# Another order for the same instructions of a one-core transformer block: per-slot scheduling settings changed for slots 0 to 9 and 18 to 31

## The chip, the core and the metric

One core of a Trainium2 chip runs the whole program. Its engines work at the same time and each takes its instructions strictly in the order in which the program lists them: TensorE (PE in the profile) multiplies matrices, ScalarE (ACT) evaluates functions, VectorE (DVE) does elementwise work, GpSimd (POOL) small extras, SyncE (SP) starts transfers. They meet at semaphores only. The metric is the device time of one execution in microseconds (us). The profile records one such execution.

## What is computed

A pre-norm attention layer and a gated feed-forward layer on 2048 tokens of width 640, with 32 heads of 20:

```python
qkv = (x @ wqkv) -> q, k, v                       # x is layernorm(A_x)
scores = einsum("bhqd,bhkd->bhqk", q, k) * 20 ** -0.5
p = softmax(scores);  o = einsum("bhqk,bhkd->bhqd", p, v)
h = A_x + o.reshape(B, S, D) @ wo
g = layernorm(h) @ w_gate;  u = layernorm(h) @ w_up      # 640 -> 1728
h2 = h + (gelu(g) * u) @ w_down
```

The only other input, `B_x`, is not read. The costly part is the softmax: 32 heads x 2048 x 2048 exponentials.

## The kernel before

**Tiles.** Scores are made transposed, 128 keys by up to 512 queries, one PSUM bank each; 2048 such tiles in all. The queries are cut into eight chunks (512, five of 256, two of 128). A *slot* is a chunk with one or more groups of four heads; there are 32 slots: 0 to 7 are the first chunk, 8 to 11 the second, and so on, 28 and 29, 30 and 31 the two short chunks at the end.

**Who takes the exponential.** ScalarE takes two or three tiles with one instruction, in 716 *units* (452 of 128x1024 and 264 of 128x1536, writing `pts` or, for the second part of the same ring of buffers, `rege`). The units alternate between PSUM banks 0 to 2 and 3 to 5. In nearly every slot three groups of four tiles, and in all 352 tiles, go to VectorE instead: a `TENSOR_SCALAR` reads a score tile from its bank (L1148), and after four tiles four more of 128x2048 (L476) make from it four terms whose sum stands for the exponential. A VectorE tile is put in the third bank of a unit that has only two ScalarE tiles (a *third bank* in the change's title), or in a free background bank, and then its score matmul is an instruction of its own behind the unit's.

**TensorE's rows.** L1267 are the score matmuls (`ps<-qt_all,kt_all`), L1212 the products of probabilities and values ("PV"; they read `pts`, `rege` or `qt_all` and `v_all`), L1051 the value projections and L902 the projections of queries and keys, L1015 a bound for the softmax, L873 (with `regw`, `wo` or `wda`) L1526 and L1613 the output projection and the feed-forward layer, L1371 a transpose. L1642 are filler matmuls with a zero operand, in groups of four, and `L476 MATMUL ps<-kt_all` another filler: the planner puts them where it expects TensorE to idle.

**VectorE's other rows.** L1059 writes projected values to `v_all`, L907 projected queries and keys, L1019 the bound, L1350 copies the finished sums of a slot out of PSUM, L1377 and L1381 normalize them, L1475, L1552 to L1618 belong to the output projection and the feed-forward layer.

**What sets the order.** Nothing in the source lists the engines' orders. Each operation is recorded with an engine, a duration, a priority and its dependencies, and a list scheduler (`Sched.schedule`) replays the program once on paper and writes down for each engine the order in which operations became startable. Score matmuls and exponentials have the highest priority, PV comes next, and projections and the feed-forward layer fill what is left. Some thresholds of the scheduler have a value for each slot, picked by `at`, which indexes the tuple with the slot of the unit that was scheduled last:

- `QK_LEAD`: how early before the current exponential ends TensorE is kept free for the next score matmuls;
- `PE_AGE`: how long an operation must have been startable before TensorE takes it though it needs another array layout than the last one;
- `SD_AGE`, `SD_ROW`: how long a VectorE tile's own score matmul is held back;
- `RESV`: how long a bank is kept free for such a tile;
- `SHUFFLE`: a number that holds some low-priority operations back by up to 1 us, and so deals the order anew.

```python
at = lambda v: v[cur] if isinstance(v, tuple) else v
```

Two more tuples are read by the planner of units, before the scheduler runs: `D_RING[t]`, out of how many of a slot's VectorE tiles the third bank may be used, and `D_FIRST[t]`, the unit with which a slot's VectorE tiles begin:

```python
nd = 4 * len(d_kb[t])
...
ring[-1] = n == 3 and (i + 1) * D_RING[t] // nd > i * D_RING[t] // nd
```

`nd` is the number of VectorE tiles of slot `t`, 12 in slots 1 to 27.

Of the kernel before, what the change touches and what calls it, by code (L numbers as in the profile page):

```python
# [18 lines left out]
DRAIN = {"pe": 0.165, "act": 0.118, "dve": 0.085, "pool": 0.05, "sp": 0.0}  # L19
WARM_WIN, WARM_MIN = 3.4, 0.5  # L20
PAD_WIN, PAD_MIN = 3.4, 0.42
QK_LEAD = (0.6, 0.68, 0.45, 0.6, 0.65, 0.68, 0.55, 0.68, 0.82, 0.55, 0.72, 0.68, 0.6, 0.72, 0.72, 0.76, 0.55, 0.55, 0.65, 0.55, 0.65, 0.65, 0.76, 0.6, 0.6, 0.5, 0.6, 0.68, 0.6, 0.72, 0.76, 0.6,)
ACT_GAP = .012
PE_AGE = (0.5, 1.5, 2.5, 8.0, 1.5, 3.0, 2.5, 0.5, 2.5, 0.5, 5.0, 3.0, 2.0, 8.0, 3.0, 0.5, 2.5, 5.0, 1.5, 5.0, 1.5, 5.0, 5.0, 5.0, 2.0, 1.0, 1.0, 3.5, 8.0, 3.0, 5.0, 1.5,)
SD_AGE = (0.3, 0.6, 1.4, 0.8, 0.2, 0.6, 0.6, 0.6, 0.3, 0.0, 0.0, 1.4, 0.6, 1.0, 0.2, 0.0, 0.3, 0.8, 0.1, 0.2, 0.2, 0.8, 0.0, 0.0, 0.0,) + (0.5,) * 4 + (0.1, 0.2, 0.3,)
SD_ROW = (0, 1.0, 1.5, 0.6, 0.6, 0.6, 1.5, 1.0, 0.3, 1.5, 1.5, 1.5, 1.0, 1.5, 1.0, 0.6,) + (1.0,) * 4 + (0.6, 0.3, 0, 1.0, 1.0, 0.6, 1.0, 0.6, 1.5, 1.5, 0.6, 1.5,)
STOP = None


# [28 lines left out]
class Sched:  # L58
# [49 lines left out]
    def schedule(self):  # L108
# [29 lines left out]
        while done < total:  # L138
# [6 lines left out]
            for e in ENGINES:  # L145
# [8 lines left out]
                while ready[e]:  # L154
                    p, i = heapq.heappop(ready[e])
                    o = ops[i]
                    got = []
                    if e == "pe" and p[0] >= 1 and at(SHUFFLE) and o.i * at(SHUFFLE) % 37 < 3 and t < o.ready + 0.999:
                        skipped.append((p, i))
# [249 lines left out]
D_SPAN = (15, 18, 17,) + (18,) * 9 + (17, 16, 18, 17, 18, 17, 18, 17, 18, 17, 17,) + (16,) * 8 + (17,)
P33 = (2, 3, 4, 5)  # L410
# [44 lines left out]
def bass_sequential_preLN__mha_block__glu_gated_geglu__prompt_kernel(  # L455
# [12 lines left out]
    with ExitStack() as es:  # L468
# [609 lines left out]
        for s_, (c, gs) in enumerate(slots):  # L1078
# [6 lines left out]
        rem = [x for x in tiles if x[1:3] not in d_kb[x[0]]]  # L1085
        n_units = [(64 - 4 * D_SLOT[s_] + D_RING[s_] * D_SLOT[s_] / max(D_SLOT[s_], 1)) / 2.5 for s_ in range(len(slots))]
        d_first = [D_FIRST[s_] if s_ and CHUNKS[slots[s_][0]][0] // 512 in (CHUNKS[slots[s_ - 1][0]][0] // 512, 3) else max(0, D_FIRST[s_])
                   for s_ in range(len(slots))]
        for _ in range(2):
# [5 lines left out]
            while left:  # L1095
# [7 lines left out]
                for t, k in ((s_, in_slot[s_]), (s_ + 1, in_slot[s_] - n_units[s_])):  # L1103
# [628 lines left out]
```

## Time and profile before

| | us |
|---|---|
| median of 3 runs (lowest, highest) | 867.15 (865.39, 867.15) |
| the profiled execution, whole | 865.97 |
| its span in the trace | 864.3 |
| ScalarE busy in the span | 828.1 (96%) |
| TensorE busy in the span | 825.5 (96%) |
| VectorE busy in the span | 734.3 (85%) |

The granted TensorE clock is full over the whole span. 1.7 us of the profiled execution lie outside its span. From 30 us to 825 us ScalarE takes one exponential after the other; before that stand the first layernorm and projections, behind it the last chunk's feed-forward layer. A row of the timeline gives start, busy time, engine, source line, operation, output and inputs, and in brackets how long the engine was idle before it and what ended that.

### The profile page before, as it was taken

The page shows a single profiled execution, that of the slowest core. Times are in us where ns is not written, and L with a number is a line of the kernel's source. Part 1 is how long each engine was busy: PE and PEld are TensorE (multiplying, and loading weights), DVE is VectorE, ACT ScalarE, POOL GpSimd, SP SyncE. Part 2 cuts the span into 40 slices and gives each one's busy share as a digit, 9 for nine tenths or more (in the row PEclk, how much of TensorE's full clock was granted, in tenths as well). Part 3 has the DMA queues.
Part 4 walks back from the last instruction along what each step waited for, and adds up shares of the span by engine and source line. Part 5 has one row for each costly group of instructions (what it writes and reads, how often), then busy time and mean ns, then how long its engine had stood idle before and what let it go on. Part 6 is the DMA issues. An engine that isn't in the chain of part 4 may idle for free.

```text
span 864.3 us, 35997 instructions
## 1 busy us (share of the span) xinstructions
PE 825.5 (96%) x16372; PEld 412.6 (48%) x16372; DVE 734.3 (85%) x1382; ACT 828.1 (96%) x794; POOL 96.0 (11%) x275
## 2 busy tenths in 40 slices
PE   8999999999999999999989999999999999999998
PEld 7442333322343444445545455445445555666667
DVE  7788999888899897878879799999999899867434
ACT  6899899999999999999999999999999999899992
POOL 8001110110002110021102110001101110010000
PEclk9999999999999999999999999999999999999999
DMA  8211132124235400012101100011002101020000
GB/s 276 77 45 53 46 85 76 52 79 98 69 116 139 119 16 6 23 43 51 44 6 32 39 26 24 10 42 37 18 16 37 46 8 31 20 48 10 3 19 17
DMA packets 52160, 43.23 MB, mean 50 GB/s; under 512 B 22660, under 2 KB 47264, under 8 KB 52008
## 3 DMA queue, kind: packets, MB, share of 16 engines
q1 hardware_dynamic: 52008, 40.93, 17.4%
q8 instruction: 129, 2.11, 1.0%
q14 instruction: 23, 0.19, 0.1%
HBM read 27.95 MB, written 10.26 MB: 44 GB/s over the span
## 4 chain that ended last, share of the span: by engine, by line
ACT 64%; PE 24%; DVE 8%; issue 0%
ACT pts L476 44%; ACT rege L476 19%; PE ps L1267 6%; PE ps L1212 5%; PE ps L873 3%; PE ps L1526 3%; PE ps L902 3%; DVE rege L476 2%; PE ps L1051 1%; DVE qt_all L476 1%; DVE rege L1148 1%; DVE qt_all L1148 1%; ACT qt_all L476 1%; PE ps L1613 1%; DVE qt_all L1564 1%; DVE regw L476 0%
## 5 line engine op out<-in xcount | busy, mean ns | idle before, releaser
L476 ACT ACTIVATE pts<-ps 128x1024 bf16<-128x1024 f32 (+1 forms) x506 | 564.3, 1260 | 6.7 <-PE ps L1212 4.4
L1267 PE MATMUL ps<-qt_all,kt_all 32*128 32x256 bf16 (+2 forms) x4096 | 286.0, 273 | 18.5 <-ACT pts L476 8.7
L476 ACT ACTIVATE rege<-ps 128x1024 bf16<-128x1024 f32 (+1 forms) x210 | 247.7, 1272 | 3.2 <-PE ps L1212 2.1
L1267 PEld LDWEIGHTS ps<-qt_all,kt_all 32*128 32x128 bf16 x4096 | 92.7, 92 | 208.7 <-ACT pts L476 117.5
L1148 DVE TENSOR_SCALAR rege<-ps 128x512 int16<-128x512 f32 x220 | 148.6, 682 | 17.0 <-PE ps L1267 16.2
L1212 PE MATMUL ps<-rege,v_all 128*21 128x256 bf16 (+2 forms) x2226 | 135.5, 287 | 1.6 <-issue 0.7
L873 PE MATMUL ps<-rege,regw 128*32 128x256 bf16 (+1 forms) x2600 | 122.5, 296 | 6.0 <-ACT rege L476 1.5
L1212 PE MATMUL ps<-pts,v_all 128*21 128x256 bf16 (+2 forms) x2414 | 120.5, 273 | 0.2
L1148 DVE TENSOR_SCALAR qt_all<-ps 128x512 int16<-128x512 f32 x132 | 89.6, 684 | 12.4 <-PE ps L1267 11.8
L476 DVE TENSOR_SCALAR rege<-rege 128x2048 int16<-128x2048 int16 x141 | 95.3, 690 | 3.9 <-PE ps L1212 3.2
L873 PEld LDWEIGHTS ps<-rege,regw 128*32 128x32 bf16 x2600 | 59.7, 96 | 39.7 <-issue 18.7
L1212 PEld LDWEIGHTS ps<-rege,v_all 128*21 128x21 bf16 x2226 | 53.2, 91 | 40.9 <-issue 22.2
L1212 PEld LDWEIGHTS ps<-pts,v_all 128*21 128x21 bf16 x2414 | 55.1, 91 | 30.0 <-issue 22.2
L873 PE MATMUL ps<-regw,rege 128*32 128x320 bf16 x1296 | 66.4, 301 | 1.1 <-DVE rege L1618 0.5
L1212 PE MATMUL ps<-qt_all,v_all 128*21 128x256 bf16 (+1 forms) x1376 | 60.9, 264 | 1.3 <-DVE qt_all L476 1.2
L476 DVE TENSOR_SCALAR qt_all<-qt_all 128x2048 int16<-128x2048 int16 (+1 forms) x98 | 60.4, 630 | 1.5 <-PE ps L1212 0.7
L902 PE MATMUL ps<-regw 128*128 128x512 bf16 x190 | 57.4, 384 | 1.0 <-DVE rege L1148 0.5
L476 POOL TENSOR_SCALAR rn<-rc 128x16 int32<-128x16 int32 x22 | 7.0, 318 | 433.6 <-DMA rc<-sums 433.5
L476 DVE TENSOR_SCALAR qt_all<-rege 128x2048 int16<-128x2048 int16 x80 | 53.7, 682 | 1.1 <-PE ps L1212 0.7
L873 PEld LDWEIGHTS ps<-regw,rege 128*32 128x32 bf16 x1296 | 29.2, 96 | 18.6 <-issue 10.8
L1526 PE MATMUL ps<-rege,regw 128*128 128x128 bf16 (+1 forms) x420 | 37.7, 238 | 0.4 <-DVE rege L1574 0.2
L476 DVE TENSOR_SCALAR rege<-qt_all 128x2048 int16<-128x2048 int16 x52 | 35.6, 685 | 0.6 <-PE ps L1212 0.4
(166 smaller groups left out, 794.9 us busy)
## 6 DMA issues: line engine op xcount, KB each, us to landing
bsum<-rsums SPq DMA_DIRECT2D x88, 64.0 KB, 2.0
rege<-in_A_x_dram SPq DMA_DIRECT2D x4, 640.0 KB, 7.1
q_rows<-regw SPq DMA_DIRECT2D x20, 128.0 KB, 1.8
out_dram<-rege SPq DMA_DIRECT2D x15, 160.0 KB, 1.9
rege<-in_A_x_dram SPq DMA_DIRECT2D x7, 320.0 KB, 3.0
regw<-in_B_w_gate_dram SPq DMA_DIRECT2D x5, 432.0 KB, 3.1
regw<-in_B_w_up_dram SPq DMA_DIRECT2D x5, 432.0 KB, 3.3
kt_all<-k_rows SPq DMA_DIRECT2D x12, 160.0 KB
```

The costliest lines, as they stand in the source:

```text
L476: return lambda eng: getattr(eng, method)(*args, **kwargs)
L873: return [lambda eng, j=j: eng.matmul(out()[32 * j:32 * j + 32], l[:, 32 * j:32 * j + 32], r, start=start, stop=stop, tile_position=(0, 32 ...
L902: w_readers.append(op("pe", lambda eng, a=a: eng.matmul(bank(bk).rearrange("p (t s) -> p t s", s=128), wqk[:, a, col + 128 * t:col + 128 * ...
L1051: w_readers.append(op("pe", lambda eng, i=i, kt=kt, a=a: eng.matmul(bank(bk)[:, i * w:i * w + w], xT[:, a, kt, 0:128], wv[:, a, 80 * g0:80 ...
L1148: d_ops.append(op("dve", lambda eng: eng.tensor_scalar(v[:, 512 * h:512 * h + 512], bank(b), EXP_MUL, -32000.0, ALU.mult, ALU.max), c_dve( ...
L1212: fns.append(lambda eng, o=nq * gs.index(g), j=j, kt=kt, g=g, pt=pt, kk=kk, st=(s_, j) not in pv_start: eng.matmul(bank(bk)[32 * j:32 * j ...
L1267: return lambda eng: eng.matmul(out()[:, kk * nq:(kk + 1) * nq], kt_all[32 * j:32 * j + 32, g, kt * 128:(kt + 1) * 128], qt_all[32 * j:32 ...
L1526: lambda eng, a=a, f=f, fi=fi: eng.matmul(bank(bk)[:, fi * nq:(fi + 1) * nq], w[:, a, F0[f]:F0[f] + 128], hnT[:, a, 128 * tb:128 * tb + nq ...
L1564: op("dve", lambda eng, bu=bu, zv=zv, uv=uv, w=w: eng.scalar_tensor_tensor(out=uv, in0=zv, scalar=1.0, in1=bank(bu, w), op0=ALU.add, op1=A ...
L1613: f == NF - 1) if cl else lambda eng, f=f, o=o, bk=bk, w0=w0, w1=w1: eng.matmul(
```

## The change

Eight tuples get other values. No operation is added or taken away by the source, no buffer and no dependency is changed.

```diff
-QK_LEAD = (0.6, 0.68, 0.45, 0.6, 0.65, 0.68, 0.55, 0.68, 0.82, 0.55, 0.72, 0.68, 0.6, 0.72, 0.72, 0.76, 0.55, 0.55, 0.65, 0.55, 0.65, 0.65, 0.76, 0.6, 0.6, 0.5, 0.6, 0.68, 0.6, 0.72, 0.76, 0.6,)
+QK_LEAD = (0.76, 0.55, 0.68, 0.68, 0.65, 0.6, 0.45, 0.5, 0.76, 0.82, 0.65, 0.68, 0.6, 0.76, 0.72, 0.76, 0.55, 0.55, 0.65, 0.5, 0.76, 0.6, 0.6, 0.6, 0.45, 0.6, 0.6, 0.68, 0.6, 0.76, 0.76, 0.6,)
-PE_AGE = (0.5, 1.5, 2.5, 8.0, 1.5, 3.0, 2.5, 0.5, 2.5, 0.5, 5.0, 3.0, 2.0, 8.0, 3.0, 0.5, 2.5, 5.0, 1.5, 5.0, 1.5, 5.0, 5.0, 5.0, 2.0, 1.0, 1.0, 3.5, 8.0, 3.0, 5.0, 1.5,)
-SD_AGE = (0.3, 0.6, 1.4, 0.8, 0.2, 0.6, 0.6, 0.6, 0.3, 0.0, 0.0, 1.4, 0.6, 1.0, 0.2, 0.0, 0.3, 0.8, 0.1, 0.2, 0.2, 0.8, 0.0, 0.0, 0.0,) + (0.5,) * 4 + (0.1, 0.2, 0.3,)
-SD_ROW = (0, 1.0, 1.5, 0.6, 0.6, 0.6, 1.5, 1.0, 0.3, 1.5, 1.5, 1.5, 1.0, 1.5, 1.0, 0.6,) + (1.0,) * 4 + (0.6, 0.3, 0, 1.0, 1.0, 0.6, 1.0, 0.6, 1.5, 1.5, 0.6, 1.5,)
+PE_AGE = (0.5, 1.5, 5.0, 1.5, 1.5, 1.0, 5.0, 2.0, 2.0, 0.5, 5.0, 3.0, 2.0, 3.5, 3.0, 0.5, 2.5, 5.0, 3.5, 3.5, 3.0, 3.0, 3.0, 5.0, 1.0, 1.5, 1.0, 3.5, 8.0, 3.5, 5.0, 1.5,)
+SD_AGE = (1.4, 0.3, 0.0, 1.0, 0.2, 0.2, 0.3, 0.6, 0.6, 0.0, 0.6, 1.4, 0.6, 1.4, 0.2, 0.0, 0.3, 0.8, 0.5, 0.3, 0.3, 0.0, 0.1, 0.6, 0.5, 0.8, 0.5, 0.5, 1.0, 1.0, 0.2, 0.3,)
+SD_ROW = (1.0, 1.0, 1.5, 0.3, 0.3, 0, 1.0, 1.5, 0.6, 1.5, 1.0, 1.5, 1.0, 1.5, 1.0, 0.6, 1.0, 1.0, 1.0, 0, 0.6, 0.3, 0.6, 1.0, 1.0, 0.3, 1.0, 0.6, 0.6, 1.5, 0.6, 1.5,)
...
-SHUFFLE = (0,) * 4 + (5, 0, 29,) + (0,) * 6 + (7, 0, 19, 0, 0, 0, 13, 0, 29, 0, 11, 19, 0, 0, 31, 11, 7, 0, 0,)
-RESV = (0.3, 0.6, 0.9, 0.0, 0.3, 0.0, 1.2, 0.6, 0.6, 0.6, 1.2, 0.0, 0.9, 0.3, 1.2, 0.0, 0.0, 0.6, 0.9, 0.0, 0.0, 1.2, 1.2, 0.3, 0.0, 0.0, 1.2, 0.3, 0.3, 0.9, 0.9, 0.6,)
+SHUFFLE = (0, 17, 0, 13, 17, 23, 5, 0, 0, 0, 7,) + (0,) * 7 + (31, 31,) + (0,) * 4 + (23, 0, 0, 31, 7, 7, 0, 0,)
+RESV = (0.6, 0.3, 0.6, 0.0, 0.9, 0.0, 1.2, 0.0, 0.0, 0.6, 0.9, 0.0, 0.9, 0.3, 1.2, 0.9, 0.0, 0.6, 0.9, 0.9, 0.9, 0.0, 1.2, 0.3, 0.0, 0.6, 1.2, 0.3, 0.3, 0.0, 0.9, 0.6,)
...
-D_RING = (12,) * 5 + (24,) * 5 + (12,) * 22
+D_RING = (12,) * 5 + (15,) * 15 + (12,) * 12
...
-D_FIRST = (8,) + (0,) * 7 + (-2,) + (0,) * 10 + (2, 0, 0, -2, 2,) + (0,) * 6 + (-2, 1,)
+D_FIRST = (8,) + (0,) * 7 + (-2,) + (0,) * 10 + (2, 0, 0, -2, 2,) + (0,) * 6 + (-2, 2,)
```

**What the planner makes of it.** With 12 VectorE tiles in a slot, `D_RING` of 12, 15 or 24 all make the condition true for every tile, and the last value of `D_FIRST` belongs to a slot without VectorE tiles. The list of units, their sizes, banks and VectorE tiles is the same before and after: 716 units, 265 of them with a VectorE tile in the third bank. Every engine has the same instructions as before, but for TensorE's fillers: 164 matmuls of L1642 become 112, and 20 of `L476 MATMUL ps<-kt_all` become 21. What moves is the order, from the middle of slot 0 to slot 29; ScalarE keeps its exponentials in the same order among themselves, and its gelu and tanh instructions stand some units earlier or later among them. SyncE's transfers move in the same way. The last 60 units have the same order on TensorE as before.

Place 1, slot 2. TensorE's rows around the first PV group of slot 2 (the three L1212 rows of 8, 14 and 2), before:

```order
L1051 MATMUL ps<-regw 128x240 x3
L1267 MATMUL ps<-qt_all,kt_all 128x512 x2
L1015 MATMUL ps<-sq,sel 32x512
L1267 MATMUL ps<-qt_all,kt_all 128x512 x2
L1051 MATMUL ps<-regw 128x240 x6
L1212 MATMUL ps<-pts,v_all 21x512 x8
L1212 MATMUL ps<-rege,v_all 21x512 x14
L1212 MATMUL ps<-pts,v_all 21x512 x2
L1051 MATMUL ps<-regw 128x240 x8
```

and now:

```order
L1051 MATMUL ps<-regw 128x240 x5
L1267 MATMUL ps<-qt_all,kt_all 128x512 x2
L1051 MATMUL ps<-regw 128x240 x8
L1267 MATMUL ps<-qt_all,kt_all 128x512
L1051 MATMUL ps<-regw 128x240 x6
L1212 MATMUL ps<-pts,v_all 21x512 x8
L1212 MATMUL ps<-rege,v_all 21x512 x14
L1212 MATMUL ps<-pts,v_all 21x512 x2
L1051 MATMUL ps<-regw 128x240 x4
```

From the program's start to this PV group there were 66 value projections of this width, and now there are 76; all else ahead of it on TensorE is the same.

On VectorE, the rows from the normalized output of slot 0 (`on<-osb,bsum`) on, before; the PV group waits for the second L1148 of the row `x2` near the end:

```order
L476 TENSOR_TENSOR on<-osb,bsum 128x512
L1148 TENSOR_SCALAR rege<-ps 128x512
L907 TENSOR_TENSOR regw<-ps,rege 128x512
...
L476 TENSOR_SCALAR rege<-rege 128x2048 x2
L476 TENSOR_SCALAR sel<-sel,kd 128x32
L476 TENSOR_SCALAR sq<-regw 128x512
L1059 TENSOR_TENSOR v_all<-ps,rs 128x2x12x20
L1019 TENSOR_SCALAR regw<-ps 32x512
L1148 TENSOR_SCALAR rege<-ps 128x512 x2
L1059 TENSOR_TENSOR v_all<-ps,rs 128x2x12x20
```

and now; the PV group waits for the second L1059 of the row `x2`:

```order
L476 TENSOR_TENSOR on<-osb,bsum 128x512
L907 TENSOR_TENSOR regw<-ps,rege 128x512
L476 TENSOR_SCALAR rege<-regw 128x2048
...
L1059 TENSOR_TENSOR v_all<-ps,rs 128x2x12x20
L1148 TENSOR_SCALAR rege<-ps 128x512 x2
L476 TENSOR_SCALAR rege<-rege 128x2048 x2
L1019 TENSOR_SCALAR regw<-ps 32x512
L1059 TENSOR_TENSOR v_all<-ps,rs 128x2x12x20 x2
L1148 TENSOR_SCALAR rege<-ps 128x512
```

Two value evictions (L1059) moved ahead of the PV group, one score tile (L1148) behind it; what the dots leave out is the same set in another order.

Place 2, slot 28. VectorE's rows from the copy of slot 27's sums (L1350) to the L1618 behind the first VectorE tiles of slot 28, before; the first PV group of slot 28 waits for the L1618:

```order
L1350 COPY osb<-ps 128x512
L1148 TENSOR_SCALAR rege<-ps 128x512 x2
L1377 RECIPROCAL rc<-ps 128x16
L476 TENSOR_SCALAR qt_all<-rege 128x2048
L1381 TENSOR_TENSOR sq<-ps,rc 128x2x80
L476 TENSOR_SCALAR rege<-rege 128x2048
L1148 TENSOR_SCALAR qt_all<-ps 128x512
L1381 TENSOR_TENSOR sq<-ps,rc 128x2x80
L1148 TENSOR_SCALAR qt_all<-ps 128x512 x3
L1618 TENSOR_TENSOR rege<-ps,rege 128x320
```

and now; the PV group waits for the second tile of the row `L1148 ... x4`:

```order
L1350 COPY osb<-ps 128x512
L1148 TENSOR_SCALAR rege<-ps 128x512 x2
L1377 RECIPROCAL rc<-ps 128x16
L1381 TENSOR_TENSOR sq<-ps,rc 128x2x80
L1148 TENSOR_SCALAR rege<-ps 128x512
L1381 TENSOR_TENSOR sq<-ps,rc 128x2x80
L476 TENSOR_SCALAR qt_all<-rege 128x2048
L1148 TENSOR_SCALAR qt_all<-ps 128x512 x4
L1618 TENSOR_TENSOR rege<-ps,rege 128x320
L476 TENSOR_SCALAR rege<-rege 128x2048
```

Of the two score tiles that stood ahead of the copy one now stands behind it; one of the two 128x2048 terms moved behind the L1618; and the PV group is let go two tiles and the L1618 earlier.

Place 3, the step from slot 11 to slot 12 (units 281 and 282). TensorE before:

```order
L1267 MATMUL ps<-qt_all,kt_all 128x256 x6
L1212 MATMUL ps<-pts,v_all 21x256 x8
L1212 MATMUL ps<-rege,v_all 21x256 x8
L873 MATMUL ps<-rege,regw 32x512 x20
L1267 MATMUL ps<-qt_all,kt_all 128x256 x12
L1212 MATMUL ps<-rege,v_all 21x256
```

and now:

```order
L1267 MATMUL ps<-qt_all,kt_all 128x256 x6
L1212 MATMUL ps<-pts,v_all 21x256 x8
L1212 MATMUL ps<-rege,v_all 21x256 x8
L1267 MATMUL ps<-qt_all,kt_all 128x256 x6
L1212 MATMUL ps<-qt_all,v_all 21x256 x8
L873 MATMUL ps<-rege,regw 32x512 x8
L1267 MATMUL ps<-qt_all,kt_all 128x256 x6
```

The twenty feed-forward matmuls between the scores of units 281 and 282 are gone from there.

**Which exponentials wait for a PV group.** An exponential overwrites a buffer that an earlier PV group has read. In most units that group stands ahead of the unit's own scores on TensorE, and the exponential waits for the scores alone. In the built order before, six of the 716 units have the group behind their scores: the 22nd, 57th, 81st, 437th, 480th and 630th. After the change they are five: the 35th, 57th, 266th, 459th and 630th.

## The prediction

> **What bounds the kernel now.** I read the page's busy times and its chain of waits first, then the table of waits for ScalarE alone from 40 to 825 us, the stretch in which it takes one exponential after the other.
>
> ```profile
> PE 825.5 (96%) x16372; PEld 412.6 (48%) x16372; DVE 734.3 (85%) x1382; ACT 828.1 (96%) x794; POOL 96.0 (11%) x275
> ACT 64%; PE 24%; DVE 8%; issue 0%
> ACT pts L476 <- PE ps L1212: 4.4, 3, 3.7
> ACT rege L476 <- PE ps L1212: 2.1, 2, 1.8
> ACT rege L476 <- PE ps L1267: 0.9, 3, 0.5
> ACT pts L476 <- PE ps L1267: 0.7, 2, 0.4
> ```
>
> ScalarE carries 64% of the chain, and its instructions are the same after the change. In those 785 us it waits 4.4 + 2.1 + 0.9 + 0.7 = 8.1 us, at ten places. The last 60 units and all behind them keep their order on TensorE, so the end can only move by what these waits become: at most 8.1 us (0.9%) can be won. 6.5 of the 8.1 us are waits for PV groups (L1212) and 1.6 for score matmuls (L1267). Where they lie:
>
> ```profile
> 52.18 1.02 ACT L476 ACTIVATE rege<-ps 128x1024 bf16<-128x1024 f32 x1 [0.26 <-PE ps L1212]
> 92.20 1.45 ACT L476 ACTIVATE pts<-ps 128x1536 bf16<-128x1536 f32 x1 [3.75 <-PE ps L1212]
> 117.34 4.20 ACT L476 ACTIVATE pts<-ps 128x1024 bf16<-128x1024 f32 x4 [0.25 <-PE ps L1212]
> 124.03 1.02 ACT L476 ACTIVATE rege<-ps 128x1024 bf16<-128x1024 f32 x1 [0.54 <-PE ps L1267]
> 334.59 3.28 ACT L476 ACTIVATE pts<-ps 128x1024 bf16<-128x1024 f32 x3 [0.38 <-PE ps L1267]
> 563.01 1.02 ACT L476 ACTIVATE pts<-ps 128x1024 bf16<-128x1024 f32 x1 [0.45 <-PE ps L1212]
> 736.80 1.02 ACT L476 ACTIVATE rege<-ps 128x1024 bf16<-128x1024 f32 x1 [1.83 <-PE ps L1212]
> ```
>
> Two places hold 5.6 us: the 57th exponential at 92.20 (first PV group of slot 2) and the 630th at 736.80 (first PV group of slot 28). Both stay in the list of exponentials that wait for a PV group, so the question is what the group itself waits for.
>
> **The change, part by part.** The setting that the title names first does nothing: the tiles in third banks are the same 265, since each of the three values of `D_RING` admits all 12. All that follows is order.
>
> *Slot 28, the 630th exponential.* VectorE's rows from the copy on, by start and busy time:
>
> ```profile
> 729.05 0.68 DVE L1350 COPY osb<-ps 128x512 f32<-128x512 f32 x1
> 729.65 0.68 DVE L1148 TENSOR_SCALAR rege<-ps 128x512 int16<-128x512 f32 x1
> 730.64 0.69 DVE L1148 TENSOR_SCALAR rege<-ps 128x512 int16<-128x512 f32 x1 [0.31 <-PE ps L1267]
> 731.25 0.25 DVE L1377 RECIPROCAL rc<-ps 128x16 f32<-128x16 f32 x1
> 731.41 0.65 DVE L476 TENSOR_SCALAR qt_all<-rege 128x2048 int16<-128x2048 int16 x1
> 731.98 0.32 DVE L1381 TENSOR_TENSOR sq<-ps,rc 128x160 bf16<-128x160 f32 x1
> 732.21 0.68 DVE L476 TENSOR_SCALAR rege<-rege 128x2048 int16<-128x2048 int16 x1
> 732.81 0.68 DVE L1148 TENSOR_SCALAR qt_all<-ps 128x512 int16<-128x512 f32 x1
> 733.41 0.31 DVE L1381 TENSOR_TENSOR sq<-ps,rc 128x160 bf16<-128x160 f32 x1
> 733.64 1.88 DVE L1148 TENSOR_SCALAR qt_all<-ps 128x512 int16<-128x512 f32 x3
> 735.44 0.48 DVE L1618 TENSOR_TENSOR rege<-ps,rege 128x320 bf16<-128x320 f32 x1
> 735.84 0.68 DVE L476 TENSOR_SCALAR qt_all<-rege 128x2048 int16<-128x2048 int16 x1
> 736.12 0.23 PE L1212 MATMUL ps<-rege,v_all 128*21 128x128 bf16 x1
> ```
>
> Steps are taken from start to start, since rows overlap at their ends. VectorE is busy from 729.05 to 735.84 with one short wait, and the PV group starts 0.28 us behind it. Now one 128x2048 term (732.21 to 732.81, 0.60), one score tile (0.60) and the L1618 (735.44 to 735.84, 0.40) stand behind the group's release: 1.60 us. The group would start at 734.5 and the exponential at 735.2, which leaves 0.23 of the 1.83 us. The moved work comes later on VectorE, where the group no longer waits for it; should its terms be late next, they hold a later PV group. Bounds: 0 (VectorE idles 1.6 us more for its tiles, whose scores wait for the banks that it frees) and -1.83. I take **-1.6**, since the order names no new wait longer than the 0.31 of the row 730.64.
>
> *Slot 2, the 57th exponential.* Here ten value projections and their two evictions moved ahead of the PV group.
>
> ```profile
> 48.00:92.00 44.00, 42.78 (x384) 16.26 (x387) 39.29 (x65) 40.16 (x39) 5.17 (x20) 1.00 0.17 45
> 92.00:128.00 36.00, 35.84 (x321) 11.74 (x313) 34.18 (x58) 35.00 (x34) 3.66 (x10) 1.00 0.24 66
> 79.42 0.69 DVE L476 TENSOR_TENSOR on<-osb,bsum 128x512 bf16<-128x512 f32 x1 [0.69 <-DMA bsum<-rsums]
> 80.89 0.69 DVE L1148 TENSOR_SCALAR rege<-ps 128x512 int16<-128x512 f32 x1 [0.77 <-PE ps L1267]
> 84.65 0.48 PE L1051 MATMUL ps<-regw 128*128 128x240 bf16 x3
> 85.39 0.69 PE L1051 MATMUL ps<-regw 128*128 128x240 bf16 x5
> 88.92 0.65 DVE L1059 TENSOR_TENSOR v_all<-ps,rs 128x480 bf16<-128x480 f32 x1
> 89.49 0.68 DVE L1019 TENSOR_SCALAR regw<-ps 32x512 bf16<-32x512 f32 x1
> 90.09 1.27 DVE L1148 TENSOR_SCALAR rege<-ps 128x512 int16<-128x512 f32 x2
> 91.29 0.64 DVE L1059 TENSOR_TENSOR v_all<-ps,rs 128x480 bf16<-128x480 f32 x1
> ```
>
> (The first two rows are windows: after the length come TensorE, its weight loads, VectorE, ScalarE and GpSimd busy, then the granted clock.) On VectorE two evictions (88.92 to 89.49, 0.57 each) come in and one tile (two of them from 90.09 to 91.29, 0.60 each) goes out: +0.54. But the wait of 0.77 at 80.89 should go, because a projection's eviction now stands there, whose matmuls are an older part of TensorE's order: -0.23 in all. On TensorE ten matmuls cost 10 x (0.69 - 0.48) / 2 = 1.05 us, and in these 44 us it idles 44 - 42.78 = 1.22 us. So either engine can just take it: **0**, between -0.9 (the wait of 0.69 for a transfer goes too) and +1.05 (the idle time can't be used). If the cover is gone the whole 1.05 is paid, since the next scores stand behind this group.
>
> *Slot 11 to 12, the 282nd exponential.* Twenty feed-forward matmuls stood ahead of its scores:
>
> ```profile
> 332.96 1.25 PE L873 MATMUL ps<-rege,regw 128*32 128x512 bf16 x20
> 334.15 0.61 PE L1267 MATMUL ps<-qt_all,kt_all 32*128 32x256 bf16 x12
> ```
>
> They take 334.15 - 332.96 = 1.19 us, and the exponential waited 0.38. They are gone from there: **-0.38** (0 at worst, if the same matmuls are late for another unit).
>
> *The small PV waits.* The 22nd, 81st, 437th and 480th exponentials waited 0.26, 0.25, 0 and 0.45 for their PV groups (the 437th has no row among the ten) and leave the list; the 35th, 266th and 459th come on it. With the mean of the old four, 0.24 each: -0.96 + 0.72 = **-0.24**, between -0.96 and 3 x 0.45 - 0.96 = +0.39.
>
> *The other waits for scores* (1.6 - 0.38 = 1.2 us at four places) are dealt anew: **0**, between -1.2 and +1.2.
>
> *Fillers, gelu, transfers.* The 52 filler matmuls less were placed in idle time; ScalarE's gelu with its two table loads stands two units earlier and takes as long there; transfers on SyncE change places by a few rows, and none of the ten waits ends with a transfer. **0**; if a key or query load should be late, that is a wait for scores like those above.
>
> ```profile
> L1642 PE MATMUL ps<-kt_all,zer 128*32 128x512 bf16 x164 | 14.4, 382 | 0.0
> PE ps L1267 <- ACT pts L476: 8.7, 28, 0.6
> ```
>
> The fillers also keep TensorE busy, and the rows speak on that: the granted clock is 1.00 in both windows above, and the longest wait of TensorE's scores for `pts` is 0.6 us.
>
> *Sum:* -1.6 + 0 - 0.38 - 0.24 + 0 = -2.2 us, against the profiled execution's own 865.97: 863.8. The median of the three runs lies 1.2 above that execution and the lowest run 0.6 below it; I add 0.4 and forecast **864.2 us**.
>
> **The rivals.**
>
> *All is dealt anew.* The waits go from the named places to others, and the sum stays near 8.1 us: 865.97 + 0.4 = 866.4. For it: TensorE is as full as ScalarE (96% each, in 92 to 128 us 35.84 of 36), so what leaves one place enters another. Against it: at slot 28 the release itself moved, not only the filling.
>
> *Third banks held by a late VectorE.* A unit whose third bank carries a VectorE tile can't begin its scores before VectorE has read that bank's last tile; the wait of 0.54 at 124.03 is of this kind. VectorE is full in slots 0 to 4 (34.18 of 36 us), and its terms and evictions are now in another order. There are 53 such units in slots 1 to 9. From nine more waits of this size on, at 0.54 each, the loss is 4.9 us, less the 2.2 won: 866.4 + 4.9 - 2.2 = 869.1, slower than before. It decides against me from about four waits on. Against it: before, only one of those units waited so long.
>
> *More is won.* If slot 2 also gets its 0.9 and the score waits halve: -2.2 - 0.9 - 0.6 = -3.7, 862.7.
>
> *TensorE slows where fillers are gone.* 52 of 164 matmuls of 14.4 us are 4.6 us of work that kept it busy. If it ran slower for want of them, and lost as much as they took, the time would be 864.2 + 4.6 = 868.8. Against it: the clock of 1.00 in every window that I read, and no wait over 0.6 us in the row on `pts`. The Trainium skill ("TensorE: Matmul & The Clock Gate", section "Part 1: The HAM clock gate") has the rule behind this: the array drops to half its clock after an idle window of about 3.4 us, so taking dummy matmuls away can cost clock. No run here shows the gate close, and no gap in the rows comes near that length.
>
> **How the numbers follow.** 0.50 for the forecast (its own range 862.4 to 866.0), 0.23 for dealt anew, 0.19 for the third banks, 0.05 for more, 0.03 for a slower TensorE. The terms' bounds added up reach from -5.3 to +2.6; that all fall on one side is unlikely, so the range takes most of both and a part of the slower cases: 861.0 to 868.3. 0.2%, about 1.7 us, is what a measurement of this kernel can tell from no change. Of the forecast's 0.50 I put 0.42 beyond that and 0.08 within: faster 0.42 + 0.05 = 0.47, same 0.08 + 0.23 = 0.31, slower 0.19 + 0.03 = 0.22.
>
> **What would show it.** In the profile after: ScalarE's wait before the exponential near 735 us at 0.1 to 0.6 us instead of 1.83; near 92 us a wait of 2.9 to 4.8; none near 334 us that ends with L1267; in the table of waits some 6 us in all from 40 to 825 us, and counts of 128x1024 and 128x1536 exponentials as before. I am wrong if the wait at slot 28 stays above 1 us, if that near 92 us grows by over 1 us, or if waits for L1267 add up to more than 3 us.

## The result, and the profile after

The changed kernel takes **863.27 us** (median of 5 runs, 862.70 to 863.97), the kernel before 867.15 (5 runs, 865.39 to 867.24): a ratio of 0.9962 with an interval of 0.9948 to 0.9977, that is 3.3 us less (2.0 to 4.5). The profiled execution after took 863.97 us with a span of 862.2, the one before 865.97 with 864.3. So the two profiles differ by 2.0 us and the medians by 3.9; whether the rest can be found is asked below.

The profile page after, busy time of each engine and the chain of waits, and then ScalarE's table of waits from 40 to 825 us (total, times, longest):

```profile
PE 825.5 (96%) x16321; PEld 412.6 (48%) x16321; DVE 733.9 (85%) x1382; ACT 827.7 (96%) x794; POOL 101.4 (12%) x275
ACT 74%; PE 20%; DVE 3%; issue 0%; POOL 0%
ACT pts L476 <- PE ps L1212: 4.3, 2, 3.5
ACT pts L476 <- PE ps L1267: 1.9, 3, 1.1
ACT rege L476 <- PE ps L1267: 0.4, 1, 0.4
ACT rege L476 <- PE ps L1212: 0.3, 1, 0.3
```

Work is the same to within 0.4 us on the three large engines, though 51 matmuls fewer are recorded. ScalarE waits 6.9 us at seven places instead of 8.1 at ten: for PV groups 4.6 instead of 6.5, for scores 2.3 instead of 1.6. Its share of the chain rises from 64% to 74%. These are the seven places, from ScalarE's timeline (start, busy time, instruction, and in brackets the wait ahead of it):

```profile
66.21 3.28 ACT L476 ACTIVATE pts<-ps 128x1024 bf16<-128x1024 f32 x3 [0.74 <-PE ps L1212]
92.56 4.20 ACT L476 ACTIVATE pts<-ps 128x1536 bf16<-128x1536 f32 x4 [3.52 <-PE ps L1212]
118.08 4.20 ACT L476 ACTIVATE pts<-ps 128x1024 bf16<-128x1024 f32 x4 [0.49 <-PE ps L1267]
405.87 3.28 ACT L476 ACTIVATE pts<-ps 128x1536 bf16<-128x1536 f32 x3 [0.31 <-PE ps L1267]
733.97 1.02 ACT L476 ACTIVATE rege<-ps 128x1024 bf16<-128x1024 f32 x1 [0.26 <-PE ps L1212]
740.13 1.45 ACT L476 ACTIVATE pts<-ps 128x1536 bf16<-128x1536 f32 x1 [1.05 <-PE ps L1267]
751.71 1.45 ACT L476 ACTIVATE rege<-ps 128x1536 bf16<-128x1536 f32 x1 [0.44 <-PE ps L1267]
```

The 630th exponential starts at 733.97 instead of 736.80 and waits 0.26 us instead of 1.83. What it waited for, in VectorE's rows and the first row of the PV group on TensorE:

```profile
731.27 0.68 DVE L476 TENSOR_SCALAR qt_all<-rege 128x2048 int16<-128x2048 int16 x1
731.87 2.48 DVE L1148 TENSOR_SCALAR qt_all<-ps 128x512 int16<-128x512 f32 x4
734.26 0.48 DVE L1618 TENSOR_TENSOR rege<-ps,rege 128x320 bf16<-128x320 f32 x1
734.66 0.68 DVE L476 TENSOR_SCALAR rege<-rege 128x2048 int16<-128x2048 int16 x1
733.29 0.23 PE L1212 MATMUL ps<-rege,v_all 128*21 128x128 bf16 x1
```

The L1618 (734.26) and the term (734.66) now come after the group began at 733.29, as the order said; it stands right behind other matmuls and waits for nothing. 6 us later something is lost again: the 635th exponential waits 1.05 us for its scores, where before's list of waits has none. Over half of that is not the order's doing. Ahead of these scores TensorE pauses for 0.38 us amid PV matmuls, and the profile shows nothing that it waits for ("issue"); in the profile of e9 (below), which has the same order, it runs through, the scores start 0.59 us earlier and the wait is 0.45. TensorE in after, then TensorE and ScalarE in e9:

```profile
739.42 0.34 PE L1212 MATMUL ps<-pts,v_all 128*21 128x128 bf16 x9 [0.38 <-issue]
739.69 0.61 PE L1267 MATMUL ps<-qt_all,kt_all 32*128 32x128 bf16 x20
```

```profile
739.10 0.61 PE L1267 MATMUL ps<-qt_all,kt_all 32*128 32x128 bf16 x20
739.54 1.45 ACT L476 ACTIVATE pts<-ps 128x1536 bf16<-128x1536 f32 x1 [0.45 <-PE ps L1267]
```

### The profile page after: what moved, and what is told of

It is laid out like the page before. It is cut to its first block, busy times and chain, and to the rows that moved or that the text cites. A ratio compares the mean times of both kernels' runs of the same rounds, so it can differ in the third digit from the quotient of the medians.

```text
span 862.2 us, 35898 instructions
## 1 busy us (share of the span) xinstructions
PE 825.5 (96%) x16321; PEld 412.6 (48%) x16321; DVE 733.9 (85%) x1382; ACT 827.7 (96%) x794; POOL 101.4 (12%) x275
## 4 chain that ended last, share of the span: by engine, by line
ACT 74%; PE 20%; DVE 3%; issue 0%; POOL 0%
ACT pts L476 50%; ACT rege L476 21%; PE ps L1267 6%; PE ps L1212 5%; PE ps L873 4%; ACT qt_all L476 2%; PE ps L902 2%; PE ps L1051 1%; PE ps L1526 1%; PE ps L1613 1%; ACT L476 1%; DVE rege L476 1%; DVE rege L1148 0%; DVE qt_all L1148 0%; DVE qt_all L476 0%
## 5 line engine op out<-in xcount | busy, mean ns | idle before, releaser
L476 ACT ACTIVATE pts<-ps 128x1024 bf16<-128x1024 f32 (+1 forms) x506 | 563.1, 1252 | 7.5 <-PE ps L1212 4.3
L1267 PE MATMUL ps<-qt_all,kt_all 32*128 32x256 bf16 (+2 forms) x4096 | 289.0, 273 | 17.4 <-ACT pts L476 8.7
L476 ACT ACTIVATE rege<-ps 128x1024 bf16<-128x1024 f32 (+1 forms) x210 | 246.4, 1270 | 0.8 <-PE ps L1267 0.4
L1148 DVE TENSOR_SCALAR rege<-ps 128x512 int16<-128x512 f32 x220 | 148.4, 683 | 20.5 <-PE ps L1267 19.9
L1212 PE MATMUL ps<-rege,v_all 128*21 128x256 bf16 (+2 forms) x2226 | 134.6, 287 | 1.7 <-DVE rege L476 1.4
L873 PE MATMUL ps<-rege,regw 128*32 128x256 bf16 (+1 forms) x2600 | 120.2, 296 | 4.7 <-ACT rege L476 1.4
L1212 PE MATMUL ps<-pts,v_all 128*21 128x256 bf16 (+2 forms) x2414 | 121.0, 273 | 1.2 <-DVE rege L1415 0.5
L476 DVE TENSOR_SCALAR rege<-rege 128x2048 int16<-128x2048 int16 x141 | 94.5, 689 | 4.5 <-PE ps L1212 3.8
L1148 DVE TENSOR_SCALAR qt_all<-ps 128x512 int16<-128x512 f32 x132 | 89.5, 684 | 8.6 <-PE ps L1267 7.9
L1212 PEld LDWEIGHTS ps<-rege,v_all 128*21 128x21 bf16 x2226 | 52.6, 91 | 39.4 <-issue 19.8
L1212 PEld LDWEIGHTS ps<-pts,v_all 128*21 128x21 bf16 x2414 | 54.8, 91 | 32.1 <-issue 23.6
L1212 PE MATMUL ps<-qt_all,v_all 128*21 128x256 bf16 (+1 forms) x1376 | 60.8, 264 | 2.5 <-DVE qt_all L476 1.9
L476 DVE TENSOR_SCALAR qt_all<-qt_all 128x2048 int16<-128x2048 int16 (+1 forms) x98 | 60.7, 631 | 1.1 <-PE ps L1212 0.4
L476 POOL TENSOR_SCALAR rn<-rc 128x16 int32<-128x16 int32 x22 | 4.8, 216 | 424.8 <-DMA rc<-sums 424.5
L476 DVE TENSOR_SCALAR qt_all<-rege 128x2048 int16<-128x2048 int16 x80 | 53.9, 685 | 0.5
L1212 PEld LDWEIGHTS ps<-qt_all,v_all 128*21 128x21 bf16 x1376 | 25.4, 91 | 23.6 <-DVE qt_all L476 10.7
```

Of the source, the lines that this page charges most:

```text
L476: return lambda eng: getattr(eng, method)(*args, **kwargs)
L873: return [lambda eng, j=j: eng.matmul(out()[32 * j:32 * j + 32], l[:, 32 * j:32 * j + 32], r, start=start, stop=stop, tile_position=(0, 32 ...
L1148: d_ops.append(op("dve", lambda eng: eng.tensor_scalar(v[:, 512 * h:512 * h + 512], bank(b), EXP_MUL, -32000.0, ALU.mult, ALU.max), c_dve( ...
L1212: fns.append(lambda eng, o=nq * gs.index(g), j=j, kt=kt, g=g, pt=pt, kk=kk, st=(s_, j) not in pv_start: eng.matmul(bank(bk)[32 * j:32 * j ...
L1267: return lambda eng: eng.matmul(out()[:, kk * nq:(kk + 1) * nq], kt_all[32 * j:32 * j + 32, g, kt * 128:(kt + 1) * 128], qt_all[32 * j:32 ...
```

## The experiments

Eight of the twelve move sets of table entries from the change to the kernel before, by slots, in the six tuples that set the order; e5 and e11 take the planner's tuples alone, and e9 and e10 thin the fillers. Each was timed beside the kernel before on the same chip, whose medians in the three sessions were 867.33 (29 runs), 867.23 (23) and 868.23 (20).

| Run | Entries of the change in slots | Median, us | Ratio to before, interval |
|---|---|---|---|
| e1 | 28, 29 | 865.17 (11) | 0.9973, 0.9962 to 0.9984 |
| e2 | 0 to 25 | 865.59 (12) | 0.9977, 0.9967 to 0.9988 |
| e3 | 0 to 9 | 866.34 (12) | 0.9991, 0.9979 to 1.0003 |
| e4 | 20 to 31 | 863.46 (6) | 0.9956, 0.9941 to 0.9971 |
| e5 | `D_RING`, `D_FIRST` only | 867.48 (12) | 0.9998, 0.9987 to 1.0010 |
| e6 | 20 to 25 | 866.68 (12) | 0.9998, 0.9988 to 1.0008 |
| e7 | 0 to 9, 20 to 31 | 863.86 (5) | 0.9958, 0.9945 to 0.9972 |
| e8 | 10 to 31 | 877.59 (4) | 1.0114, 1.0096 to 1.0132 |
| e9 | all, fewer fillers | 864.40 (5) | 0.9959, 0.9945 to 0.9973 |
| e10 | none, fewer fillers | 867.79 (11) | 0.9993, 0.9984 to 1.0003 |
| e11 | `D_RING` only | 867.66 (10) | 0.9998, 0.9989 to 1.0007 |
| e12 | 2 to 9, 20 to 31 | 886.84 (4) | 1.0211, 1.0194 to 1.0227 |

**e1 and e2: slots 28 and 29 alone, and all but these.** The whole edit of e1 is seven numbers:

```diff
-QK_LEAD[29], PE_AGE[29], RESV[29] = 0.72, 3.0, 0.9
+QK_LEAD[29], PE_AGE[29], RESV[29] = 0.76, 3.5, 0.0
-SD_AGE[28:30], SD_ROW[28], SHUFFLE[28] = (0.5, 0.1), 1.5, 11
+SD_AGE[28:30], SD_ROW[28], SHUFFLE[28] = (1.0, 1.0), 0.6, 7
```

> The kernel before with only the entries of slots 26 to 31 from the change; TensorE's order is that of before up to just ahead of slot 28. Theory of separate places: ScalarE starts units 1 to 629 as before (within 0.2 us), the wait of 1.83 us ahead of the 630th exponential shrinks to about 0.3, and some 0.8 comes back at the 635th, which now waits about 1 us for its scores: start of the 631st exponential -1.6 us, of the 716th -0.8 to -1.0, time about 0.9 us less (ratio 0.999). Rival, all of the gain lies here: 3.3 us less (0.996). Rival, dealt anew: the 716th starts within 0.3 us of before.

e2 is the changed kernel with these seven set back.

> The changed kernel with the entries of slots 26 to 31 set back. Theory of separate places: up to the 629th exponential as in the changed kernel (start -1.2 us against before), then the wait of 1.83 us ahead of the 630th is back, no wait of 1 us ahead of the 635th: the 716th starts 1.2 us earlier than before, time 1.2 us less (ratio 0.9986). Rival, all of the gain lies in slots 26 to 31: no change (1.000). Rival, dealt anew: the wait at the 630th doesn't come back as it was, but another does elsewhere.

Three of ScalarE's rows from the 630th exponential on, of e1 and, last, the 630th of e2:

```profile
734.66 1.02 ACT L476 ACTIVATE rege<-ps 128x1024 bf16<-128x1024 f32 x1 [0.26 <-PE ps L1212]
740.23 1.45 ACT L476 ACTIVATE pts<-ps 128x1536 bf16<-128x1536 f32 x1 [0.45 <-PE ps L1267]
754.96 4.70 ACT L476 ACTIVATE pts<-ps 128x1536 bf16<-128x1536 f32 x4 [0.73 <-PE ps L1267]
```

```profile
735.97 1.02 ACT L476 ACTIVATE rege<-ps 128x1024 bf16<-128x1024 f32 x1 [1.82 <-PE ps L1212]
```

The seven numbers take the wait from 1.83 to 0.26, and setting them back brings it back at 1.82: the place is what the prediction said it was. What follows differs: in e1 the 635th waits 0.45, not the expected 1, and later ones wait up to 0.73, all for scores. In the timings e1 wins 2.3 us (1.4 to 3.3), more than the 0.9 expected, and e2 2.0 (1.0 to 2.9), where 1.2 was expected. "All of the gain lies here" fits e1 and not e2; "dealt anew" does not fit the place, which answers to the seven numbers both ways. The profiles show less than the timings: the 716th exponential starts 0.82 us earlier than before in e1, as said, but in e2 at 838.79, 0.14 later than before, where 1.2 earlier was expected. That points at the reference, which e11 takes up.

**e3, e4, e6, e7: where else the gain lies.** The edits are slices; of e4, for one tuple of the six:

```diff
-QK_LEAD[20:32] = (0.65, 0.65, 0.76, 0.6, 0.6, 0.5, 0.6, 0.68, 0.6, 0.72, 0.76, 0.6)
+QK_LEAD[20:32] = (0.76, 0.6, 0.6, 0.6, 0.45, 0.6, 0.6, 0.68, 0.6, 0.76, 0.76, 0.6)
...
```

> The kernel before with only the entries of slots 0 to 9 from the change. Theory of separate places: as the changed kernel up to about the 255th exponential (35th waits about 0.8 us more, the waits at 22, 81 and 86 are gone: start -0.5 us), after that the waits of before: 282nd waits 0.4, 437th and 480th as before, 630th 1.8. Time 0.5 us less (0.9994). Rival, the early slots hold the gain (VectorE is fullest there): 2 us less (0.998). Rival, dealt anew: some wait over 0.5 us appears later that neither kernel has, and the time is not below before.

> The kernel before with only the entries of slots 20 to 31 from the change. Theory of separate places: as before up to the 430th exponential, then the changes of the late slots: the 480th waits 0.2 to 0.4 us less, the 630th 1.6 less, the 635th about 1 more: the 716th starts 1.0 to 1.4 us earlier than before (ratio 0.9985). Together with slots 0 to 9 it should then give the 2.0 us of the changed kernel's profile. Rival, the median's 3.3 us is more than the profile's waits explain: 2 us or more from this half alone.

> The kernel before with only the entries of slots 20 to 25 from the change. Slots 20 to 31 gave 3.8 us (0.9956), slots 26 to 31 alone 2.3 us (0.9973). Theory of separate places: what is left, 1.5 us (0.998), from the wait ahead of the 480th exponential (0.45 before, gone or under 0.2) and smaller ones up to the 629th, with the wait of 1.83 us ahead of the 630th as before. Rival, the late gain is one gain that either part brings (whatever changes the filling ahead of slot 28): 2.3 us or more here too, and the wait ahead of the 630th shrinks although its own entries are those of before.

> The kernel before with the entries of slots 0 to 9 and 20 to 31 from the change, 10 to 19 as before. Theory of separate places: the late gain of 3.8 us and 0 to 0.8 of the early slots: 862.7 to 863.5, ratio 0.995; the 282nd exponential waits 0.4 again. Rival, the middle carries part of the changed kernel's gain: 865 or more (0.9975).

Slots 20 to 31 alone (e4) give 3.8 us (2.5 to 5.1), as much as the whole change. The theory of separate places had 1.0 to 1.4, so it missed, and e4's rival came true: the gain is more than the profile's waits explain. In e7 slots 0 to 9 add nothing to it that shows (863.86, just above the expected 862.7 to 863.5). By themselves slots 0 to 9 give 0.8 (-0.3 to 1.8) and slots 20 to 25 0.2 (-0.7 to 1.0), neither told from nothing; for e6 the theory had 1.5 and missed again. e1's 2.3 and e6's 0.2 fall short of e4's 3.8, but within the intervals. In e6 the wait ahead of the 630th stayed at 1.83, so its rival, that any other filling ahead of slot 28 brings the gain, falls. Its profile is 1.13 us ahead of before at the 629th exponential and loses that behind the 630th, where it takes 34.62 us from the 631st to the 660th and before 33.20. For the changed kernel's median the middle, slots 10 to 19, is not needed. (The change has entries there in slots 10, 13, 15, 18 and 19; the title leaves out 10, 13 and 15.)

**e8 and e12: the same entries, another mixture, much slower.** e8 leaves slots 0 to 9 as before; e12 is e7 without slots 0 and 1:

```diff
-QK_LEAD[2:10] = (0.45, 0.6, 0.65, 0.68, 0.55, 0.68, 0.82, 0.55)
+QK_LEAD[2:10] = (0.68, 0.68, 0.65, 0.6, 0.45, 0.5, 0.76, 0.82)
...
```

> The changed kernel with the entries of slots 0 to 9 set back. Theory of separate places: the late gain of 3.8 us, the wait of the 282nd gone (0.4) and 0.4 lost again near the 346th: 863.5, ratio 0.9955; the wait of the 35th exponential is gone, and the 57th waits 3.7. Rival, dealt anew (the list of waits for PV groups is another here: 22, 57, 81, 544, 608, no 630): the waits move to other places and the sum from 40 to 825 us stays at 7 to 8 us, time 865 or more.

> The kernel before with the entries of slots 2 to 9 and 20 to 31 from the change: e7 without slots 0 and 1. In its order 350 L1526 and 112 L1613 matmuls stand behind the last scores, where before, the changed kernel and e7 have 210 and 56, and e8, which lost 11.6 us behind its last exponential, had 289 and 112. Theory, what isn't fitted in as filling is paid at the end: 140 x 0.057 + 56 x 0.148 = 16.3 us more from the last exponential to the end (41.9 instead of 25.6), time 881 to 886. Rival, only the waits of ScalarE count (slots 0 and 1 alone were dropped from e7): 863 to 867.

e8 lost 9.9 us (8.3 to 11.4), far more than the rival's waits (9.5 us from 40 to 825 us, instead of 8.1) could cost. Its last exponential starts only 1.3 us later than before, but its end is 37.2 us behind that instead of 25.6. The last exponential of before and of e8, then TensorE's groups by shape: after, from 836.6 us to its end, and e8, from 840 us to its end:

```profile
838.65 1.19 ACT L476 ACTIVATE pts<-ps 128x1024 bf16<-128x1024 f32 x1
```

```profile
839.99 1.17 ACT L476 ACTIVATE pts<-ps 128x1024 bf16<-128x1024 f32 x1
```

```profile
L1526 PE MATMUL ps<-rege,regw 128*128 128x128 bf16 x207 | 12.6, 219 | 0.0
L1613 PE MATMUL ps<-regw,rege 128*128 128x320 bf16 x28 | 4.1, 299 | 0.1
```

```profile
L1526 PE MATMUL ps<-rege,regw 128*128 128x128 bf16 x280 | 16.3, 219 | 0.0
L1613 PE MATMUL ps<-regw,rege 128*128 128x320 bf16 x84 | 12.4, 299 | 0.0
```

73 and 56 matmuls more, 3.7 + 8.3 = 12.0 us: work of the feed-forward layer that otherwise fills TensorE's gaps between scores was not fitted in and is done behind the last exponential, where nothing hides it. The 73 belong to the last chunk but one, the 56 to the chunk ahead of that; in the kernel before, those 56 start between 810.1 and 828.6 us, in e8 between 842.5 and 852.3. e12 tests this: its order has 140 and 56 more there. It was to lose 16.3 us behind the last exponential, and the rival said it would be 863 to 867. It took 886.84, 0.8 above the expected 881 to 886; the last exponential starts at 841.84 and the span ends at 887.0, 45.2 behind it, so 19.6 more than before:

```profile
841.84 1.25 ACT L476 ACTIVATE pts<-ps 128x1024 bf16<-128x1024 f32 x1
```

```profile
L1526 PE MATMUL ps<-rege,regw 128*128 128x128 bf16 x280 | 16.9, 219 | 0.2 <-ACT rege L755 0.2
L1613 PE MATMUL ps<-regw,rege 128*128 128x320 bf16 x84 | 11.7, 299 | 0.1
L1526 PE MATMUL ps<-rege,regw 128*128 128x256 bf16 x65 | 8.5, 273 | 0.0
```

The mechanism held. It is 3.3 us more than expected because 65 of the matmuls are twice as wide, 8.5 / 65 = 0.131 us each where 0.057 was taken (4.8 us in all; the 56 of L1613 took 7.6 instead of 8.3). Its waits from 40 to 825 us add up to 13.8 us, and its last exponential starts 3.2 us later than before's. One of these waits stands at the 630th exponential, although e12 has the seven numbers of e1:

```profile
739.12 1.02 ACT L476 ACTIVATE rege<-ps 128x1024 bf16<-128x1024 f32 x1 [2.68 <-PE ps L1212]
```

So the entries of slots 28 and 29 remove that wait behind the orders of before and after, and not behind every order of the earlier slots.

**e5 and e11: the ring alone, and one order seen three times.**

```diff
-D_RING = (12,) * 5 + (24,) * 5 + (12,) * 22
+D_RING = (12,) * 5 + (15,) * 15 + (12,) * 12
```

> The kernel before with D_RING and D_FIRST of the change and no other entry. Theory: the order on every engine is that of before, so this is before once more: ratio 1.000 within 0.2%, the same ten waits of ScalarE, and its spread of single runs is as wide as that of before (865.2 to 870.7 in 29 runs). Its profile is a second look at one order: where it differs from that of before, that is what executions of one order differ by. Rival, the title's sentence holds (tiles move between third banks): other waits at slots 5 to 19, ratio 0.998 or below.

> The kernel before with D_RING alone of the change; the order is that of before, so this is a third profile of one order. Its median should be 867.3 within 0.5 us. Open is why both profiled executions (865.97, 865.45) lay 1.3 to 1.9 us under the median. Theory: chance, executions of one order differ by waits that come and go; then this profile has, where it is longer, waits of ScalarE between the 196th and the last exponential that the other two lack. Rival: what unprofiled executions lose lies at the start or the end (start of the first exponential, or the 25.6 us from the last exponential to the end).

(e5 also has the last value of `D_FIRST`.) Nothing moved, in the order or in the time: 0.9998 twice. So these are a second and a third profile of before's order, at 865.45 and 866.92 us. ScalarE's rows that begin with the 631st and with the 660th exponential, of before, e5, e11 (with its waits from the 630th on) and after:

```profile
737.72 5.93 ACT L476 ACTIVATE pts<-ps 128x1536 bf16<-128x1536 f32 x5
770.92 5.67 ACT L476 ACTIVATE pts<-ps 128x1024 bf16<-128x1024 f32 x5
```

```profile
737.46 5.75 ACT L476 ACTIVATE pts<-ps 128x1536 bf16<-128x1536 f32 x5
770.39 5.67 ACT L476 ACTIVATE pts<-ps 128x1024 bf16<-128x1024 f32 x5
```

```profile
736.71 1.02 ACT L476 ACTIVATE rege<-ps 128x1024 bf16<-128x1024 f32 x1 [1.83 <-PE ps L1212]
737.63 3.28 ACT L476 ACTIVATE pts<-ps 128x1536 bf16<-128x1536 f32 x3
741.25 2.56 ACT L476 ACTIVATE pts<-ps 128x1024 bf16<-128x1024 f32 x2 [0.34 <-PE ps L1267]
752.21 1.45 ACT L476 ACTIVATE pts<-ps 128x1536 bf16<-128x1536 f32 x1 [0.58 <-PE ps L1267]
771.50 1.15 ACT L476 ACTIVATE pts<-ps 128x1024 bf16<-128x1024 f32 x1
```

```profile
734.89 4.19 ACT L476 ACTIVATE pts<-ps 128x1536 bf16<-128x1536 f32 x4
768.78 5.64 ACT L476 ACTIVATE pts<-ps 128x1024 bf16<-128x1024 f32 x5
```

The wait of 1.83 us comes in every look. But from the 631st to the 660th exponential one order takes 33.20, 32.93 and 33.87 us: the small waits for scores in slots 28 and 29 come and go. The changed kernel took 33.89 there, and 34.82 in the profile of e9, which has its order. Over all profiles but those of e8 and e12, seven with the old entries of slots 28 and 29 take 32.9 to 34.6 us, 33.7 on average, and five with the new ones 33.5 to 34.8, 34.0 on average. So what the 1.66 us won at the 630th cost behind it is 0.3 us on average, which can't be told from nothing; the 0.7 that before and after show side by side is one draw.

This does not explain why the timings show more than the profiles. Four profiles of before's order (e10 below has it too) took 865.45 to 866.92 us, 866.2 on average, and two of the changed order (after and e9) 863.97 and 864.85, 864.4 on average: 1.8 us, where the timings say 3.3 (2.0 to 4.5). The four lie 0.7 to 2.0 us under the medians of their runs, the two 0.7 and 0.5 above. So some 1.5 to 2 us of the gain is a difference that the profiled executions don't show, most of it time that the other executions of the old order lose; where they lose it stays open. The granted clock does not explain it: the 59 of before's 72 executions at a full clock have a median of 867.26 us, and the 13 that showed 0.998 one of 869.0.

**e9 and e10: the fillers.** The scheduler puts one filler where four stood; the order of all else is unchanged.

```diff
-o.fns, o.mode, o.deps = self.pad(live_bank), "col", set()
+o.fns, o.mode, o.deps = self.pad(live_bank)[:1], "col", set()
...
-o.fns = o.fns + self.pad(o.pvb)
+o.fns = o.fns + []
```

> The changed kernel with the same order on every engine, but one filler matmul (L1642) where a group of four stood: about 28 instead of 112. Theory of the prediction (fillers stand in idle time and cost and bring nothing): as the changed kernel, 863.3 us, ratio 0.996, every execution at a granted clock of 1.000. Rival, the fillers hold the clock (in the profile of e8 the clock was 0.50 for some 3.2 us behind an idle time of TensorE of 1.65 us): some executions show 0.998 or less, each such window costs 1.3 to 2.5 us, and the median is 1 us or more above 863.3.

> The kernel before, same order, one filler where four stood: about 41 instead of 164. Of the kernel before, some one in seven executions showed a clock of 0.998, at 868.0 to 870.7 us against a median of 867.3. Theory of the prediction: 867.3 us, ratio 1.000. Rival, the fillers hold the clock: more than one in three executions at 0.998 or less, 1 us or more above before (0.1% to 0.4% slower).

The filler group in e9, which was x112 with 11.1 us in the changed kernel:

```profile
L1642 PE MATMUL ps<-kt_all,zer 128*32 128x512 bf16 x27 | 9.7, 382 | 0.0
```

With 85 fillers less the changed kernel keeps its ratio (0.9959 after 0.9962) and all five executions a clock of 1.00; the rival's loss of 1 us isn't there. The four of a group run side by side on TensorE (112 matmuls of 382 ns took 11.1 us), so a quarter of the matmuls still takes 9.7 of the 11.1 us: the run thins the fillers, and a kernel without that time wasn't tried. Before's order with 40 fillers is not slower either; four of its eleven executions showed a clock of 0.998, against 13 of 72 of the kernel before. Four of eleven is the share that its rival named, more than one in three, but too few to tell more from the same, and its median lost nothing that shows.

## Why the prediction was right, point by point

- **`D_RING` does nothing:** shown (e5, e11).
- **Slot 28, -1.6 us:** right in place and size. ScalarE was 1.17 us ahead of before at the 629th exponential and 2.83 at the 630th, 1.66 more; e1 and e2 show that the entries of slots 28 and 29 do it, behind either kernel's order (not behind e12's). The sentence that later terms "hold a later PV group" should they be late next was priced at 0, and no run shows it: TensorE's rows from the 630th exponential to the scores of the 635th have no wait for VectorE. TensorE is full there (busy 5.00 of the 5 us from 733 to 738), and the 635th's scores come 0.45 us late in e9 and 1.05 in after, with the pause of 0.38.
- **Slot 2, 0:** the 57th waits 3.52 us instead of 3.75 and starts 0.36 later, because the 35th lost more than that before it. VectorE's waits of 0.69 and 0.77 near 80 us went, as said. Cover was there: TensorE is busy 43.27 of the 44 us from 48 to 92, where it was 42.78, and VectorE 39.64 instead of 39.29.

```profile
48.00:92.00 44.00, 43.27 (x385) 16.47 (x388) 39.64 (x66) 40.16 (x39) 5.78 (x20) 1.00 0.17 45
```

- **The 282nd, -0.38:** no wait is left there; ScalarE was 0.37 us ahead of before at the 281st and 0.92 at the 282nd.
- **The small PV waits, -0.24:** the 22nd, 81st and 480th lost 0.26 + 0.25 + 0.45, the 35th got 0.74: -0.22. The 266th and 459th wait for nothing that shows.
- **The other score waits, 0:** this was the mis-sized term. 1.2 us were left by the prediction, 2.29 are there (0.49, 0.31, 1.05, 0.44): +1.1, inside its bounds, and nearly all of it is the 635th. On average over four looks at the old order (before, e5, e10, e11) and two at the new (after, e9) all waits for scores are 1.9 and 2.45 us, which leaves +0.9. The 0.49 is the 81st again, which now waits for its scores.
- **Fillers, gelu, transfers, 0:** ScalarE's instructions were put down as the same, and it is busy 0.4 us less (827.7 after 828.1). So the step "the end can only move by what these waits become" was not quite right.
- **The sum.** In the two profiles -2.2 was predicted and -2.0 came, in part by luck: the table of waits shrank by 1.2 only, from 8.1 to 6.9 where "some 6" was forecast, and the rest is the 0.4 of busy time and some 0.4 of idle time that the table doesn't list. In the timings 3.3 came (2.0 to 4.5), 3.9 between the medians, so 2.2 is at the low end; e4 (2.5 to 5.1) has it outside. That the forecast of 864.2 lies only 0.9 above the median is luck too: it started from 865.97 + 0.4 = 866.4, 0.8 below before's median of 867.15, and the two errors partly cancel. From median to median the same sum gives 865.0. What the timings show beyond the profiles is not located.
- **The rivals.** "Dealt anew" with the same sum fell: the waits from 40 to 825 us are 6.9 and 7.2 us in two looks at the new order, and 7.9 to 9.1 in four at the old one. A late VectorE holding third banks has no trace in slots 1 to 9 beyond 0.49 us at 118.08. Slower for want of fillers has nothing for it: 52 fillers less in the changed kernel, 137 less in e9, and the clock stayed, though the fillers that were left still took 9.7 of 14.4 us. The prediction had that no run shows the clock drop; e8 and e12 do, behind stretches that these orders don't have (last section). What the prediction did not have among its rivals is how a new order really gets slower here, e8 and e12: the last 60 units kept their order, and that was taken as a reason for the end to stay; it holds only since the same matmuls were left behind them.

None of the variants beats the changed kernel beyond the intervals; e4 and e7 equal it.

## What to carry to other kernels

When only the order changes, first count in it what stands behind the last instruction of the bounding engine: 56 matmuls more there cost about 8 us, while no wait changed by 2 us from before to after. Then read the waits of the bounding engine place by place, and look a few units further for what a removed wait brings next. And look several times at one order, old and new: a single wait differed by 0.6 us and a stretch of thirty exponentials by 0.9 between profiles of one order, and timings can hold a part of the gain that no profile shows.

## What the hardware showed that was not expected

TensorE's clock fell in the profiled executions of e8 and e12. TensorE's windows in e8 (busy time and count, granted clock, DMA share and rate), with the matmul that ended its idle time and the exponential that paid:

```profile
533.00:534.00 1.00, 0.00 (x0) 1.00 0.39 114
535.00:536.00 1.00, 1.00 (x24) 0.82 0.02 5
536.00:537.00 1.00, 1.00 (x19) 0.50 0.14 42
539.00:540.00 1.00, 1.00 (x30) 0.97 0.00 0
532.24:535.65 3.41, 1.65 (x40) 1.00 0.22 62
```

```profile
534.40 0.50 PE L1212 MATMUL ps<-pts,v_all 128*21 128x256 bf16 x9 [1.65 <-DVE rege L1574]
539.47 1.02 ACT L476 ACTIVATE pts<-ps 128x1024 bf16<-128x1024 f32 x1 [1.28 <-PE ps L1267]
```

By the two partial windows the clock was half from 535.64 to 539.06, for 3.4 us, and ScalarE then waited 1.28 us for its scores. The idle time ahead of it was 1.65 us. The Trainium skill ("TensorE: Matmul & The Clock Gate", section "Part 1: The HAM clock gate") gives an idle window of about 3.4 us as what closes the gate; here half of that was enough, and the half clock lasted about one such window. In the 3.4 us ahead of the half clock TensorE was busy for 1.65 us, a share of 0.48. e12 shows the same once more: 1.48 busy of 3.41 us (0.43), then half a clock for 3.4 us. The emptiest 3.4 us of before had 0.62 and kept the full clock; after has none under 0.62 either, and both had a clock of 1.00 in every 10 us from 45 to 838 us. First e12, then before:

```profile
466.23:469.64 3.41, 1.48 (x35) 1.00 0.61 173
469.64:473.06 3.42, 3.42 (x49) 0.50 0.02 5
```

```profile
317.40:320.81 3.41, 2.13 (x42) 1.00 0.00 0
```

So in these runs the clock fell behind 3.4 us with a busy share of 0.43 and 0.48 and stayed at 0.62; where between them it turns was not measured. Half a clock for 3.4 us takes 0.2% off the mean over 865 us, as much as an execution with a clock of 0.998 lacks.
